# A recurrence and a highway layer on one core: two zero matmuls fewer, late outputs in other buffers, a new order of work

## The chip, the cores and the metric

The kernel runs on one core of a Trainium2 chip. The metric is device time in microseconds, the median of several executions. A core has five engines with a queue of instructions each: TensorE (PE, matmuls and transposes; PEld are its weight loads), VectorE (DVE), ScalarE (ACT), GpSimd (POOL) and SyncE (SP), which here only issues transfers. Each queue runs in its own order, and engines wait for one another by semaphores. Matrix results land in PSUM, everything else lies in SBUF.

## The reference, cut to what matters

Two steps on 4 sequences of 6336 tokens with 256 channels, in float32:

```python
sig = 1 / (1 + exp(-f_logit))
f = lower_bound + (1 - lower_bound) * sig
i = 1 - f
h = 0                                     # per sequence and channel
for t in range(S):
    h = f[:, t] * h + i[:, t] * x[:, t]   # a recurrence along the tokens
    y[:, t] = h
y = y.reshape(B * S, D)
H = maximum(y @ w_h, 0)
T = 1 / (1 + exp(-(y @ w_t + b_t)))
out = T * H + (1 - T) * y
```

Logits and x are read and the output is written once, about 26 MB each.

## The kernel before

**Units.** The 25344 tokens are cut into 28 units in the order of the tokens: units 0 and 1 of 256 tokens, 2 of 512, then 23 of 1024 (3 to 25), 26 of 512 and 27 of 256. A unit is worked in two halves of 128 channels, with channels on the partitions and tokens along the free dimension, so that the recurrence is one scan instruction per half. At a sequence's start inside a unit the scan is cut in two.

**Steps of a unit**, each a function named do_ and a letter:

- `l` and `x` load the logits and x (SP queue, 1 MB each for a full unit); six buffers each.
- `u` (ACT) takes the sigmoid of the negated logits. `b0` to `b3` (POOL, or DVE where the token has a `v`) multiply u and x, two blocks of 128 tokens at a time.
- `i` (PE) transposes u, `f` (ACT, or DVE with `v`) makes the decay from it out of PSUM. `p` (PE) transposes b.
- `s` (DVE) is the scan: it reads f and p's PSUM bank, and the last column of the scan before.
- `z` and `g` (PE) are the two matrix products. `t` (ACT) is the sigmoid of z; `d` (DVE) takes the maximum of g and the scaled y. In the kernel's algebra the weights are scaled and w_h has the identity taken off, so that the output is y scaled by `diag` plus d times t.
- `E` (POOL, pieces of 512 columns) and `e` (DVE, the rest) multiply d and t. A unit's last number says how many columns go to POOL; of a full unit's 2048 the rest goes to DVE. A POOL product is made to wait for the DVE product ahead of it, since the two share a port.
- `o` (PE) transposes back and adds, four blocks of 128 tokens at a time; `c` (ACT, or DVE with `v`) copies it to SBUF, into one of four `o` buffers of 512 KB; `w` (SP) stores it.

At the start, `pc` and `cc` turn the parameters, `wh` and `wt` load the weights, into the first `o` buffer, `WS` or `WSv` takes the identity off w_h (POOL or DVE), `WHa` and `WTa` scale the weights on ACT, `dga` makes `diag`.

**PSUM.** Two single banks (a0, a1) serve `i` and `p`; three pairs of banks (b0 to b2) serve `z`, `g`, `o`. The number behind a token's colon is its buffer. A step that takes a buffer waits for the last reader of what was in it.

**Order.** Nothing is scheduled at build time: the list `order`, a string of some 870 tokens, is read from left to right, and each token puts its instructions at the end of its engine's queue, in program order. A token `k*16` puts 16 matmuls on zeros, whose result nobody reads, into PE's queue; `p3.1*2` puts two of them ahead of that step. Eight more stand at the very start (line 178), behind a memset. The list and the units' shares come from a planner outside the kernel, so the text of the list is the whole of the schedule.

The lines of the steps: loads 281, u 293, b 301, i 307, f 316 (DVE) and 318 (ACT), p 327, scan 344, z and g 356 with 141 for the matmuls that keep their weights, t 369, d 373, e and E 378, o 397 and 398, c 405 (DVE) and 407 (ACT), w 412.

Of the kernel before, what the change touches and what calls it, by code (L numbers as in the profile page):

```python
# [77 lines left out]
g1.1:1 f4.1:4 z2.0:0 s3.0 d1.1 E2.1:1 u5:0 E1.0:2 x6:0 p4.1:0 o0.0:2 t2.0 c0.0:1 i5.0:1 z3.0:0 f5.0:1 l7:1 b5.1:2 w0.0
g3.1:1 o1.0:2 b5.0 t3.0:0 l8:2 b5.3 p4.0:1 b5.2 c1.0:2 u6:1 s4.1:0 i5.1:0 E2.0 d3.1:3 z3.1:2 b6.2:0 b6.0 f5.1:0 t3.1
s4.0 g3.0:1 d3.0 p5.1:1 i6.0:0 f6.0:3 z4.0:0 b6.1 w1.0 o2.0:2 p5.0:0 s5.1:1 i6.1:1 t4.0:1 c2.0:3 b6.3 g4.1:0 u7:2 x7:1  # L80
s5.0 z4.1:1 d4.1:0 E3.0:0 f6.1:4 l9:3 e3 g5.0:2 E3.1 d5.0:1 w2.0 g4.0:0 p6.1:1 i7.0:0 t4.1 b7.1:1 b7.0 b7.2 d4.0
z5.1:2 u8:0 E4.2:2 o3.0:1 s6.1:2 l10:4 f7.0:2 c3.0:0 p6.0:0 o3.1:0 b7.3 s6.0 z5.0:1 x8:2 t5.1:2 e4 E4.1 c3.1:1 u9:1
g5.1:2 i7.1:0 x9:3 E4.0 z6.0:0 w3.0 d5.1 p7.0:1 o4.1:2 t5.0 E5.1:1 b8.2:2 f7.1v:0 o4.0:1 p7.1:0 t6.0:0 b8.1 b8.0
c4.1:2 s7.0:3 c4.0:3 g6.0:2 z6.1:1 u10:2 g6.1:0 t6.1 b8.3 i9.0:1 s7.1 d6.0:2 i8.0:0 g7.0:1 d6.1 f9.0:1 i8.1:1 z7.1:2
z7.0:0 f8.0:4 E5.0 b9.2:0 w3.1 i10.1:0 x10:4 f8.1:3 d7.0:3 e5 e6:0 p8.0:1 o5.0:1 w4.0 t7.1:1 b9.1 b9.0 o6.1:2 f10.1:2
b9.3 p8.1:0 w4.1 t7.0 c6.1:0 s8.0:0 g7.1:0 c5.0:1 i10.0:1 l11:5 E7.0:2 E6.0 b10.1:1 o5.1:2 f10.0:0 i9.1:1 c5.1:3 s8.1
p9.0:0 z8.0:1 x11:5 b10.0 f9.1:4 b10.3 d7.1 u11:0 b10.2 s9.0:1 z8.1:2 p9.1:1 s9.1 o6.0:0 t8.0:2 l12:0 t8.1 g8.1:1
g9.0:2 w6.1 u12:1 c6.0v:2 E7.1 i11.1:1 z9.0:0 d9.0:0 i12.0:0 w5.0 f11.1:3 t9.0:0 p10.0:1 z9.1:2 g9.1:0 f12.0:1 E7.2
b11.0:2 d8.1:1 t9.1 w5.1 E7.3 i11.0:0 b11.3 o7.1:1 s10.0:2 f11.0:4 d9.1 l13:1 b11.1 p10.1:1 i12.1:0 s10.1 c7.1:0
g8.0:2 o7.0:1 b11.2 p11.0:1 u13:2 x12:0 d8.0 E9.0:1 l15:2 f12.1:0 b12.1:0 z10.0:0 s11.0:3 c7.0:1 t10.0:1 g10.1:2  # L90
g10.0:1 w6.0 z10.1:0 E9.1 x13:1 w7.1 d10.0:2 i13.0:1 E9.3 u15:0 p11.1:0 E9.2 t10.1 b12.0 l14:3 b12.3 d10.1 b12.2
b13.2:1 w7.0 x15:2 f13.0:2 s11.1 o9.0:1 e8:0 o9.1:2 i13.1:1 c9.0:3 p12.0:0 x14:3 e10:2 l17:4 b13.1 c9.1:2 f13.1:4
z11.0:1 o8.0:2 o8.1:0 p12.1:1 u14:1 c8.0:0 w9.1 z11.1:2 c8.1:1 s12.0:1 b13.0 b13.3 i14.0:0 s12.1 g11.0:0 i15.1:1
b15.1:2 t11.0:0 b15.0 f14.0:3 w9.0 b14.2:0 p13.0:0 z12.1:1 d11.0:3 t11.1 s13.0:0 f15.1:1 g11.1:2 d11.1 i15.0:1 g12.0:0
t12.1:2 b14.0 f15.0:0 l16:5 w8.0 p13.1:0 z12.0:2 w8.1 u17:2 t12.0 b14.1 o10.1:1 E11.1:1 E11.0 b14.3 x16:4 i14.1:1
E11.2 d12.0:0 s13.1 g12.1:0 g13.0:2 c10.1:2 E12.0:0 f14.1:2 o10.0:1 E11.3 p14.0:0 d12.1 b15.3 b15.2 g13.1:0 u16:1
l18:0 i16.1:1 c10.0:3 d13.0:1 o11.0:2 E12.2 w10.1 s14.0:2 z13.0:1 f16.1:4 b16.0:1 c11.0:0 w10.0 p14.1:0 d13.1 t13.0:1
i16.0:1 z13.1:2 x17:5 E13.0:2 f16.0:3 s14.1 o11.1:0 e12 p15.1:1 b16.2 t13.1 i17.1:0 b16.3 c11.1:1 E12.1 z14.0:1 b16.1
g14.0:2 w11.0 E13.1 f17.1:2 z14.1:0 s15.1:3 l19:1 E13.2 t14.0:0 p15.0:0 w11.1 d14.0:2 g14.1:1 t14.1 i17.0:1 s15.0
u18:0 x18:0 f17.0:1 o12.1:2 c12.1:2 E13.3 o12.0:0 E14.1:1 p16.0:0 p16.1:1 d14.1 o13.0:1 s16.0:1 g15.1:2 s16.1 b17.2:0  # L100
c12.0:3 c13.0:0 u19:1 g15.0:0 l20:2 i18.0:0 b17.1 d15.1:3 b17.3 e14 b17.0 f18.0:0 z15.0:1 i19.0:1 t15.0:2 i19.1:0
b18.0:2 E14.0 x20:1 g16.1:2 d15.0 f19.1:3 d16.1:0 o13.1:1 w12.1 p17.0:0 w13.0 f19.0:4 z16.1:0 g16.0:2 p17.1:1 c13.1:1
b18.1 t16.1:1 b18.3 b18.2 x19:3 s17.0:0 z15.1:1 i18.1:0 o14.1:0 u20:2 b20.2:1 d16.0 f18.1:1 t15.1 o14.0:2 p18.1:0
s17.1 z17.1:1 c14.0:2 i20.0:1 z16.0:2 l21:3 c14.1:0 t17.1:0 w13.1 e15:0 f20.0:2 g17.1:0 b20.1 z17.0:1 s18.1:2 t16.0
w12.0 p18.0:1 b20.3 t17.0 w14.0 u21:0 i20.1:0 d17.1:1 s18.0 b19.2:0 w14.1 b19.1 g17.0:2 o15.0:1 g18.0:0 d17.0 f20.1:1
b20.0 l22:4 x21:2 i21.1:1 d18.0:2 l23:5 c15.0:1 b19.0 b19.3 o15.1:2 p19.0:0 f21.1:0 e16:2 z18.0:0 E17.1:1 w15.0
p19.1:1 c15.1:3 o16.1:1 s19.0:3 z18.1:2 i21.0:0 s19.1 w15.1 E17.3 t18.0:2 c16.1:2 E17.2 g18.1:0 g19.0:1 E16.0 t18.1
o16.0:2 d18.1 p20.1:1 f21.0:4 E17.0 E18.0:0 d19.0:3 u22:2 c16.0:0 z19.0:0 p20.0:0 z19.1:1 x22:4 o17.0:2 b21.1:2
s20.1:1 b21.3 t19.0:1 b21.0 w16.1 l24:0 b21.2 o17.1:0 i22.0:1 t19.1 s20.0 e18 E19.0:2 E19.1 b22.0:0 p21.0:0 b22.3
u23:1 g19.1:1 c17.0:1 s21.0:0 b22.1 z20.0:2 c17.1:3 z20.1:0 d19.1 f22.0:3 i23.1:0 t20.0:0 x23:5 p21.1:1 g20.0:2  # L110
o18.0:1 w17.0 f23.1:1 b22.2 t20.1 c18.0:2 i22.1:0 g20.1:0 f22.1:2 w17.1 o18.1:1 s21.1 l25:1 d20.0:0 p22.0:1 d20.1
i23.0:0 w18.0 g21.1:2 E19.3 s22.0:2 x24:0 u24:0 E19.2 f23.0:4 o19.1:0 i24.1:1 b23.3:1 b23.1 c19.1:1 d21.1:1 p22.1:0
z21.0:2 g21.0:0 w19.1 e20:1 f24.1:0 s22.1 c18.1:3 w16.0 b23.0 b23.2 t21.0:2 o19.0:1 E20.2 p23.0:1 w18.1 E20.0 d21.0
g22.0:2 E20.1 z21.1:0 s23.0:3 b24.1:2 u25:2 c19.0:2 b24.3 x25:1 l27:2 i25.1:0 z22.0:1 f25.1:3 d22.0:2 t22.0:1 w19.0
x26:3 p23.1:1 i24.0:0 z22.1:2 g22.1:1 t21.1 t22.1 s23.1 b24.0 o20.0:0 d22.1 l26:3 b24.2 f24.0:2 o20.1:2 c20.1:1 e21:0
E21.0 p24.1:0 c20.0:0 E22.2:2 b25.2:0 z23.1:1 b25.0 w20.1 g23.1:2 p24.0:1 z23.0:0 s24.1:1 d23.1:3 t23.1:0 t23.0 b25.3
o21.1:1 g23.0:2 i25.0:0 s24.0 b25.1 o21.0:0 u27:1 E22.0 w20.0 d23.0 c21.1:3 g24.1:1 i27.0:1 f25.0:4 w21.1 c21.0:2
# [335 lines left out]
```

## Time and profile before

| what | value |
|---|---|
| median of 3 executions | 210.8 us (210.74 to 211.06) |
| the profiled execution | 211.13 us |
| its span (first to last instruction) | 209.3 us |
| busy: PE, DVE, ACT, POOL | 192.9, 193.1, 194.9, 174.8 us |
| moved by DMA | 78.69 MB, 376 GB/s over the span |
| granted TensorE clock | 0.994 |

A line of a timeline gives the start in us, the duration, the engine, the source line, the operation with output and inputs, their shapes and how many instructions were merged; in square brackets stands how long the engine was idle before it and what ended that. Tile names are those of the program without buffer numbers, so which unit a line belongs to follows from the list's order. A line of a stretch gives its limits, its length, the busy us of PE, PEld, DVE, ACT and POOL with their number of instructions, the granted clock, the busy share of the 16 transfer engines and their rate. The slices on the page are 40 equal parts of the span, 5.23 us each, in tenths of busy time.

### The profile page before, as it was taken

The page shows a single profiled execution, that of the slowest core. Times are in us where ns is not written, and L with a number is a line of the kernel's source. Part 1 is how long each engine was busy: PE and PEld are TensorE (multiplying, and loading weights), DVE is VectorE, ACT ScalarE, POOL GpSimd, SP SyncE. Part 2 cuts the span into 40 slices and gives each one's busy share as a digit, 9 for nine tenths or more (in the row PEclk, how much of TensorE's full clock was granted, in tenths as well). Part 3 has the DMA queues.
Part 4 walks back from the last instruction along what each step waited for, and adds up shares of the span by engine and source line. Part 5 has one row for each costly group of instructions (what it writes and reads, how often), then busy time and mean ns, then how long its engine had stood idle before and what let it go on. Part 6 is the DMA issues. An engine that isn't in the chain of part 4 may idle for free.

```text
span 209.3 us, 4671 instructions
## 1 busy us (share of the span) xinstructions
PE 192.9 (92%) x1827; PEld 132.6 (63%) x1827; DVE 193.1 (92%) x149; ACT 194.9 (93%) x194; POOL 174.8 (84%) x168
## 2 busy tenths in 40 slices
PE   7978799999998999889999999999989899999981
...
DVE  0489999999999999999999999999999999999842
ACT  4889899999999999999999999999999999997871
...
DMA  6999999999999999999999999999999999756585
GB/s 238 387 421 421 418 417 420 417 423 418 409 427 402 399 386 418 430 408 423 428 357 377 426 411 425 411 403 399 419 421 344 332 368 345 293 205 232 193 340 223
DMA packets 15982, 78.69 MB, mean 376 GB/s; under 512 B 1748, under 2 KB 2264, under 8 KB 10072
## 3 DMA queue, kind: packets, MB, share of 16 engines
...
q8 instruction: 14, 0.23, 0.5%
q14 instruction: 8, 0.07, 0.1%
...
## 4 chain that ended last, share of the span: by engine, by line
PE 32%; DVE 24%; issue 4%; ACT 3%; DMA 3%; DVEq 0%; ACTq 0%
DVE y L344 14%; DVE d L373 8%; PE g L356 5%; PE bT L327 4%; PE op L398 4%; PE g L141 4%; PE op L397 4%; PE z L356 4%; PE z L141 4%; PE uT L307 3%; DMA out_dram<-o 3%; DVE e L378 2%; ACT o L407 1%; ACT u L293 1%; ACT f L318 0%
## 5 line engine op out<-in xcount | busy, mean ns | idle before, releaser
L301 POOL TENSOR_TENSOR bv<-u,x 128x512 bf16<-128x512 f16 x95 | 108.6, 1173 | 13.9 <-DVE e L378 7.6
L344 DVE TENSOR_TENSOR_SCAN y<-f,y,bT 128x1024 bf16<-128x1024 f16 (+5 forms) x54 | 106.7, 1991 | 1.4 <-PE bT L327 1.0
L378 POOL TENSOR_TENSOR e<-d,t 128x512 bf16<-128x512 bf16 (+1 forms) x60 | 65.9, 1118 | 9.8 <-DVE e L378 7.3
L373 DVE SCALAR_TENSOR_TENSOR d<-y,ncc,g 128x1024 bf16<-128x1024 bf16 (+2 forms) x56 | 62.8, 1142 | 3.8 <-PE g L356 3.4
L369 ACT ACTIVATE t<-z,bt 128x1024 bf16<-128x1024 f32 (+2 forms) x56 | 57.2, 1043 | 1.7 <-PE z L141 0.9
L318 ACT ACTIVATE f<-uT,ncc 128x1024 f16<-128x1024 f16 (+2 forms) x53 | 55.5, 1060 | 2.1 <-PE uT L307 1.9
L293 ACT ACTIVATE u<-l 128x2048 f16<-128x2048 f32 (+2 forms) x28 | 48.5, 1732 | 3.3 <-DMA l<-in_f_logit_dram 3.3
L407 ACT COPY o<-op 128x1024 f32<-128x1024 f32 (+1 forms) x49 | 48.5, 1019 | 1.8 <-DMA out_dram<-o 0.6
L398 PE MATMUL op<-ident_b,e 128*128 128x128 bf16 x396 | 48.7, 219 | 0.8 <-DVE e L378 0.8
L397 PE MATMUL op<-diag,y 128*128 128x128 f16 x396 | 48.7, 219 | 0.4 <-ACT o L407 0.4
L398 PEld LDWEIGHTS <-e 128*128 128x128 bf16 x396 | 44.1, 113 | 4.1 <-issue 1.1
L397 PEld LDWEIGHTS <-y 128*128 128x128 bf16 x396 | 44.2, 113 | 2.4
L356 PE MATMUL z<-y,w_sb 128*128 128x512 bf16 (+1 forms) x112 | 39.2, 367 | 1.5 <-ACT o L407 0.6
L356 PE MATMUL g<-y,w_sb 128*128 128x512 bf16 (+1 forms) x112 | 39.4, 368 | 1.0 <-ACT t L369 0.6
L327 PE MATMUL bT<-ident_f,bv 128*128 128x128 f32 x198 | 32.1, 278 | 4.4 <-DVE y L344 2.3
L141 PE MATMUL g<-y,w_sb 128*128 128x512 bf16 x92 | 34.8, 379 | 0.0
L141 PE MATMUL z<-y,w_sb 128*128 128x512 bf16 x92 | 34.8, 379 | 0.0
L307 PEld LDWEIGHTS <-u 128*128 128x128 f16 x396 | 26.1, 98 | 13.2 <-issue 5.6
L307 PE MATMUL uT<-ident_h,u 128*128 128x128 f16 x396 | 30.9, 220 | 3.1 <-ACT f L318 1.3
L356 PEld LDWEIGHTS <-w_sb 128*128 128x128 f16 x224 | 21.7, 98 | 17.4 <-issue 1.2
L141 PEld LDWEIGHTS <-w_sb 128*128 128x128 f16 x184 | 17.9, 97 | 18.6 <-issue 4.1
L327 PEld LDWEIGHTS bT<-ident_f,bv 128*128 128x128 f32 x198 | 22.0, 141 | 11.2 <-POOL bv L301 3.4
...
## 6 DMA issues: line engine op xcount, KB each, us to landing
...
l<-in_f_logit_dram SPq DMA_DIRECT2D x23, 1024.0 KB, 10.2
...
```

What stands on the lines that cost most here:

```text
L141: return pe.add_instruction(mybir.InstMatmult(name=nc.get_next_instruction_name(), start_tensor_calc=start, stop_tensor_calc=stop, tile_si ...
L301: shared(pin(e.tensor_mul(st[n]["bv"][:, k].rearrange("p d j -> p j d"), st[n]["u"][:, q:q + 2], st[n]["x"][:, q:q + 2])), not eng)
L307: pin(nc.tensor.transpose(uT[:, j * P:(j + 1) * P], st[n]["u"][:, j, h * P:(h + 1) * P], ident_h))
L318: pin(nc.scalar.activation(to, of, AF.Identity, scale=ncc[:, h:h + 1], bias=1.0))
L327: pin(nc.tensor.transpose(words[:, k:k + g * (P - 1) + 1:g], pair, ident_f))
L344: pin(nc.vector.tensor_tensor_scan(y[:, c:e], st[n]["f", h][:, c:e], st[n]["bT", h][:, c:e], 0.0 if fresh else carry[h], op0=ALU.mult, op1 ...
L356: pin(nc.tensor.matmul(p[:, a:e], w, half(n, "y", ki)[:, a:e], start=ki == 0, stop=ki == NH - 1))
L369: pin(nc.scalar.activation(half(n, "t", m), st[n]["z", m][:, :tokens(n)], AF.Sigmoid, bias=bt[:, m:m + 1]))
L373: pin(nc.vector.scalar_tensor_tensor(half(n, "d", m), half(n, "y", m), ncc[:, m:m + 1], st[n]["g", m][:, :tokens(n)], op0=ALU.mult, op1=AL ...
L378: shared(pin(eng.tensor_mul(st[n]["e"][:, a:e], st[n]["d"][:, a:e], st[n]["t"][:, a:e])), eng is nc.gpsimd)
L397: pin(nc.tensor.matmul(o, half(n, "y", h)[:, cols], diag[:, h], start=True, stop=False))
L398: pin(nc.tensor.matmul(o, half(n, "e", h)[:, cols], ident_b, start=False, stop=True))
```

## The change

Three things change.

1. At line 178 six matmuls on zeros stand where eight stood.
2. A buffer number in the list may now be a name. `c23.1:x3` puts its output into buffer 3 of x's six. The copies of units 23 to 27 do so: c23.1 to x3, c23.0 to x5, c24.0 to x0, c24.1 to x1, c25.0 to x4, c25.1 to x2, c26.0 to x5, c27.0 to x3. Such an output tile has x's full size, of which the copy and the store use the first half at most. Earlier units keep the four `o` buffers.
3. The list is another one, and so are the columns that POOL takes of each unit's product: 27392 in all instead of 29440. The units and their sizes stay. Of the steps that may run on two engines: `WSv` becomes `WS` (DVE to POOL); b1.0 and b3.0 go from DVE to POOL; f0.1 goes from DVE to ACT, f1.0 and f2.0 from ACT to DVE; on DVE stand the copies c1.0 and c25.0 where c6.0 and c27.0 stood. The loads' order at the start goes from l0 l3 wh x0 l1 l2 x1 wt x2 x3 l4 x4 l5 to l0 l3 x0 l1 wh l2 x1 x2 x3 wt l4 x4 l5. The matmuls on zeros in the list are 26 instead of 24.

The diff, with the list cut to its start and end:

```diff
     units = [
         (0, 128, 2, 0, 'y', 4, 512),
-        (0, 128, 2, 256, 'y', 4, 512),
+        (0, 128, 2, 256, 'y', 4, 0),
         (0, 128, 4, 512, 'y', 4, 1024),
...
-        (0, 128, 8, 21504, 'y', 4, 1280),
-        (0, 128, 8, 22528, 'y', 4, 256),
-        (0, 128, 8, 23552, 'y', 4, 1536),
+        (0, 128, 8, 21504, 'y', 4, 2048),
+        (0, 128, 8, 22528, 'y', 4, 1280),
+        (0, 128, 8, 23552, 'y', 4, 0),
         (0, 128, 4, 24576, 'y', 4, 512),
         (0, 128, 2, 25088, 'y', 4, 256),
     ]
     order = """
-l0:0 pc:0 l3:1 wh:0 cc u0:0 u3:1 i0.1:0 i0.0:1 k*16 x0:0 l1:2 f0.1v:0 f0.0:1 l2:3 WSv b0.0v:0 u1:2 p0.0:1 x1:1 p0.1:0
-k*3 s0.1:0 WHa s0.0 i1.1:0 k*3 u2:0 wt f1.1v:2 i1.0:0 x2:2 i2.1:1 f1.0:3 b1.0v:1 f2.1:4 g0.1:1 x3:3 b2.1:2 p1.0:0 b2.0
-i3.1:1 l4:4 WTa s1.0:1 p1.1:0 s1.1 g0.0:2 d0.0:0 d0.1 z0.1:0 f3.1:0 i3.0:0 i2.0:1 z1.1:2 t0.1:0 b3.2v:0 f2.0:1 z0.0:0
-p2.1:1 b3.0v f3.0:3 z1.0:1 p2.0:0 t0.0 b3.1 x4:4 s2.1:2 g1.0:0 b3.3 t1.1:1 s2.0 p3.1*2:1 u4:2 dga l5:5 E0.0:0 x5:5
+l0:0 pc:0 l3:1 u0:0 i0.0:0 x0:0 i0.1:1 k*12 cc f0.1:0 l1:2 wh:0 f0.0:1 l2:3 x1:1 x2:2 b0.0v:0 WS p0.1:0 u3:1 u1:2
+p0.0:1 k*2 s0.0:0 i3.1:1 s0.1 i1.0:0 k*2 f1.0v:2 x3:3 i1.1:0 k*3 WHa f3.1:3 f1.1v:4 b1.0:1 u2:0 p1.0:1 g0.0:1 s1.0:1
+p1.1:0 k*2 i3.0:1 g0.1:0 s1.1 wt i2.0:0 g1.0:2 f3.0:1 i2.1:1 b2.0:2 WTa f2.1:0 b2.1 d0.0:0 f2.0v:2 p2.0:0 z1.1*2:1
+d0.1 b3.0:0 b3.1 g1.1:0 p2.1:1 t1.1:0 l4:4 x4:4 d1.0:1 s2.0:2 z1.0:2 d1.1 b3.2v dga z0.1:1 t1.0 u4:2 z0.0:0 t0.1:1
+s2.1 b3.3 p3.1*3:0 l5:5 t0.0 i4.0:1 f4.0:4 e1:0 b4.0:1 b4.3 g2.1:2 g2.0:1 z2.1:0 i4.1:1 t2.1:2 b4.1 s3.1:3 x5:5 p3.0:0
...
-t25.0:1 i26.0:1 z25.1:1 i27.1:0 E23.1 d25.1:1 E23.2 d25.0 w22.1 f26.0:2 e24 p26.0:1 t25.1 o23.1:2 o23.0:0 f27.1:4
-x27:2 p26.1:0 o24.0:1 c23.1:3 o24.1:2 E25.0:2 b27.0:2 s26.0:2 c23.0:2 p27.0:1 s26.1 g26.1:0 c24.0:1 c24.1:0 g26.0:1
-e25 p27.1:0 z26.0:2 w23.1 t26.0:0 E25.2 E25.1 d26.1:2 d26.0 z26.1:0 o25.0:1 w23.0 t26.1 c25.0:3 s27.1:3 o25.1:2 s27.0
-g27.0:0 z27.1:1 E26.0:1 w24.0 d27.0:3 e26 z27.0:0 c25.1:2 t27.0:2 o26.0:2 t27.1 g27.1:1 d27.1 E27.0:0 w24.1 w25.0 e27
-w25.1 c26.0:1 w26.0 o27.0:0 c27.0v:0 w27.0
+c22.0:2 s25.0 E23.1 o22.1:1 g24.1:2 i26.1:1 f26.0:1 p26.0:0 c22.1:3 d24.0:0 f26.1:0 g25.0:1 d24.1 b27.0:0 E23.2
+p26.1:1 w21.1 w21.0 z25.1:0 z25.0:2 t25.1:1 d25.0:1 o23.1:1 s26.0:2 t25.0 o23.0:0 g25.1:2 w22.0 E24.0:1 s26.1 c23.1:x3
+p27.0:1 c23.0:x5 e24 g26.0:1 E24.2 w22.1 i27.1:0 d25.1 o24.0:0 d26.0:2 f27.1:4 z26.0:2 c24.0:x0 E24.1 p27.1:0 t26.0:0
+o24.1:1 e25:0 z26.1:0 w23.0 w23.1 w24.0 E26.0:2 s27.0:3 c24.1:x1 o25.0:2 o25.1:1 t26.1 s27.1 w24.1 g26.1:0 c25.0v:x4
+w25.0 c25.1:x2 d26.1 z27.0:2 z27.1:1 g27.0:0 t27.0:2 w25.1 e26 o26.0:2 d27.0:3 t27.1 c26.0:x5 g27.1:1 d27.1 E27.0:1
+e27 w26.0 o27.0:0 c27.0:x3 w27.0
 """
...
-        return pool.tile(shape, dtype, tag=f"{name}{slot}", name=name)
+        return pool.tile(shape, dtype, tag=slot if str(slot)[:1].isalpha() else f"{name}{slot}", name=name)
...
-    for _ in range(8):
+    for _ in range(6):
         nc.tensor.matmul(once["idle"][:, :512], zeros[:, :P], zeros, start=True, stop=True)
...
-        o = sb([P, 4, D], FP32, "o", slot)
+        o = sb([P, NB if slot[:1] == "x" else 4, D], FP32, "o", slot)
```

More of the change, by code (lines that the diff above doesn't have):

```diff
@@ L78 @@
[L78 to L117, printed above, removed]
@@ new lines @@
+E3.2 z4.1:1 b6.2 f7.0:1 u8:0 d4.1:1 w1.0 s5.0 l10:4 o2.0:0 b6.0 c2.0:3 i6.1:1 f6.1:2 i7.1:0 x10:3 x9:4 g5.1:0 w2.0
+i6.0:1 d4.0 t4.1 f6.0:4 z5.0:1 f7.1v:0 b7.2:1 d5.1:0 e4:1 p6.0:0 e3 l11:5 i8.1:1 u9:1 o3.0:0 l12:0 b7.0 b7.1 b7.3
+o3.1:2 s6.0:2 E4.0 f8.1:3 b8.1:2 t5.0:2 c3.0:0 p6.1:1 g5.0:1 i9.0:0 c3.1:2 s6.1 z6.1:0 p7.1:1 d5.0 w3.1 o4.0:2 f9.0:4
+p7.0:0 u10:2 c4.0:1 w4.0 b8.0 t6.1:0 g6.0:1 s7.1:3 i8.0:1 z5.1:2 d6.0:2 f8.0:2 E4.1 z6.0:0 i10.1:1 b8.2 g6.1:1 t5.1
+s7.0 b8.3 o4.1:2 t6.0 E5.0:2 E5.1 e5 p8.1:0 f10.1:0 c4.1:3 i9.1:1 d6.1 w3.0 b9.2:0 z7.1:0 g7.0:1 s8.1:1 d7.0:3 f9.1:1
@@ new lines @@
+g12.0:2 E12.2:0 o10.0:1 c10.1:2 f15.0:1 g13.0:0 b16.2:1 d12.0 i16.1:1 w8.0 w8.1 p14.0:0 c10.0:3 x17:5 z13.0:1 E12.1
+E12.0 o11.1:2 f16.1:3 d13.0:1 b16.3 p14.1:1 s14.0:2 l18:0 u17:1 z13.1:0 t13.0:1 i17.1:0 E12.3 w10.1 b16.1 b16.0
+c11.1:0 t13.1 g13.1:1 s14.1 f17.1:2 d13.1 o11.0:2 w10.0 l20:1 p15.0:1 g14.1:0 i16.0:0 s15.0:3 b17.0:2 c11.0:1 z14.1:1
+z14.0:2 p15.1:1 f16.0:4 p16.0:0 E13.1:1 b17.1 d14.1:2 o12.0:0 t14.1:0 b17.2 s15.1 w11.1 E13.0 g14.0:1 b17.3 t14.0
+o12.1:2 u18:0 d14.0 i17.0:1 c12.0:2 E13.2 f17.0:1 l19:2 w11.0 s16.0:0 E14.2:2 x18:0 w12.0 c12.1:3 g15.0:1 g15.1:0
```

58 lines of the change are left out of this document (43 added, 15 removed).

## The prediction

> **What bounds the kernel now.** I read the page first, then the stretches of the span, then the timeline of each engine at the two ends, and last the groups by form, which give the durations. On the page, the slices say that four engines and the transfers are full at once, and that only the ends are not.
>
> ```profile
> PE   7978799999998999889999999999989899999981
> DVE  0489999999999999999999999999999999999842
> ACT  4889899999999999999999999999999999997871
> DMA  6999999999999999999999999999999999756585
> ```
>
> The stretches (busy us of PE, PEld, DVE, ACT, POOL, then clock, transfer share, GB/s) make it sharper: in the body VectorE and ScalarE do not miss a tenth of a microsecond, and in the last ten VectorE falls to 2.09 of 5 while the transfers are busy again.
>
> ```profile
> 120.00:130.00 10.00, 9.65 (x105) 7.04 (x103) 10.00 (x8) 10.00 (x10) 9.18 (x9) 1.00 1.02 419
> ...
> 195.00:200.00 5.00, 4.93 (x58) 3.67 (x57) 4.42 (x7) 4.20 (x6) 4.60 (x5) 1.00 0.69 266
> 200.00:205.00 5.00, 3.65 (x50) 2.90 (x47) 2.09 (x5) 3.92 (x6) 1.48 (x2) 1.00 0.91 362
> ```
>
> So the time is: start of the unbroken VectorE work, plus that work, plus its holes in the tail, plus the last store. The head on the timeline (start, duration, engine, line):
>
> ```profile
> 7.69 0.78 DVE L301 TENSOR_TENSOR bv<-u,x 128x512 bf16<-128x512 f16 x1 [1.86 <-DMA x<-in_x_dram]
> ...
> 10.75 0.73 DVE L301 TENSOR_TENSOR bv<-u,x 128x512 bf16<-128x512 f16 x1
> ...
> 12.09 0.75 DVE L344 TENSOR_TENSOR_SCAN y<-f,y,bT 128x256 bf16<-128x256 f16 x1 [0.61 <-PE bT L327]
> 12.43 2.29 POOL L301 TENSOR_TENSOR bv<-u,x 128x512 bf16<-128x512 f16 x2 [4.55 <-DMA x<-in_x_dram]
> ...
> 19.00 2.34 DVE L344 TENSOR_TENSOR_SCAN y<-f,y,bT 128x1024 bf16<-128x1024 f16 x1
> ```
>
> From 12.09 (s1.0) inputs no longer hold VectorE; 19.00 is s3.1, the first full-size scan. The tail, VectorE first, then ScalarE:
>
> ```profile
> 197.84 1.41 DVE L373 SCALAR_TENSOR_TENSOR d<-y,ncc,g 128x512 bf16<-128x512 bf16 x2 [0.58 <-PE g L356]
> ...
> 201.55 0.48 DVE L373 SCALAR_TENSOR_TENSOR d<-y,ncc,g 128x256 bf16<-128x256 bf16 x1 [1.02 <-PE g L356]
> ...
> 204.15 0.48 DVE L373 SCALAR_TENSOR_TENSOR d<-y,ncc,g 128x256 bf16<-128x256 bf16 x1 [1.79 <-PE g L356]
> ...
> 205.58 0.69 DVE L405 COPY o<-op 128x512 f32<-128x512 f32 x1 [0.55 <-PE op L398]
> ```
>
> ```profile
> 200.55 1.02 ACT L407 COPY o<-op 128x1024 f32<-128x1024 f32 x1 [0.41 <-DMA out_dram<-o]
> 201.78 1.01 ACT L407 COPY o<-op 128x1024 f32<-128x1024 f32 x1 [0.21 <-DMA out_dram<-o]
> ```
>
> VectorE's holes there are 0.58 + 1.02 + 1.79 + 0.55 and 0.1 between d27.1 and e27, 4.05 in all; two of ScalarE's are output copies waiting for an output buffer still being stored.
>
> **Account of the profiled execution.** Span 209.3: s3.1 at 19.0; VectorE work and its 0.15 of small holes; the 4.05; 3.03 from the end of the last copy (206.27) to the end. Work is thus 209.3 - 19.0 - 0.15 - 4.05 - 3.03 = 183.07. This execution took 211.13, so 1.83 lies around the span, and it is 0.33 above the median 210.8; I carry the difference over to 210.8.
>
> **Part 1, amounts.** Counting the list's tokens by form with the means of the groups by form, VectorE goes from 202.46 to 202.78 us (two bv of 0.74 go to GpSimd, one f of 512 comes from ScalarE at about 0.76, the e shares grow by 1.04), ScalarE from 213.04 to 212.35, GpSimd from 178.5 to 176.4. (These exceed the busy time because neighbours overlap by 0.07 to 0.1.) Zero matmuls: 8 + 24 become 6 + 26, no change in number. The transfers and their 78.4 MB stay.
>
> **Part 2, head.** Landings follow bytes queued ahead: with the page's 238, 387 and 421 GB/s per slice of 5.23 us, the queue has moved 1.24, 3.27 and 5.47 MB at 5.2, 10.5 and 15.7 us, and x0 (1.83 MB through it) landed 0.94 later than that, x2 (3.67 MB) 1.0 later. In the new issue order x0 has 1.57 MB: 7.0 instead of 7.69. wh moves from 7.01 to 8.4, wt, now behind x2 and x3, from 11.1 to 14.9, x2 from 12.43 to 11.75, x3 to 14.2; x1 keeps 2.88 MB and lands at 10.4 in both. So the first scans start 0.7 earlier, and that gain dies at s1.0: its b1.0 is moved to GpSimd (1.17 instead of 0.73), behind WS there, 10.4 to 11.6, and with the 0.6 that before took from bv to scan, s1.0 starts at 12.05 against 12.09. VectorE idles about 1.7 before it. From there to s3.1: s1.0, s1.1, d0.0, f2.0v, d0.1, d1.0, s2.0, d1.1, b3.2v, s2.1, e1 = 1.35 + 0.4 + 0.69 + 0.8 + 1.2 + 0.4 + 0.68 + 1.2 + 0.36 = 7.1, and 0.15 for d1.1: PE stands at z1.1 until ScalarE's WTa, waiting for wt, ends at 15.8, and g1.1 comes after. s3.1 at 19.3: **+0.3**. Ends: -0.3 (x1's landing is the estimate that carries it) and +0.8 (d1.1 and s2.1 each late by PE's queue behind z1.1, where p2.1 also stands). VectorE work behind s3.1 is 0.16 more (192.02 against 191.86): **+0.16**. ScalarE reaches u4 at 17.8 instead of 17.26, but u5 must wait for l5, at 23.49 in both; its work left is then the same (179.9 after u5), so its lateness is covered by that landing.
>
> Six zero matmuls instead of eight let prmT go 0.85 earlier (0.43 each in the row 1.19 to 4.78); f0.1 and f0.0 then fit in ScalarE's 2.25 wait for l3. If that cover fails, it costs ScalarE 0.3 ahead of l5, still hidden. What eight may have bought is the clock: the zero matmuls ran 0.43 apart, those from 5.31 on 0.23 apart. The Trainium skill (TensorE: Matmul & The Clock Gate, Part 1) says that the clock opens only after a busy window of about 3.4 us, which runs freely, so a thinner start may open it a window later. The sum by that page would have k*12 take 12 x 0.43 = 5.2 instead of 2.7 us, ending near 9.7. By rows of this case alone: even at 0.43 apart to the end of k*12, p0 would slip by under 2 us, s0 by as much, and 1.7 of it falls in the hole before s1.0. I take 0, with 0.3 as the other end.
>
> **Part 3, tail.** From s25.1 VectorE has 18.55 us to e27 in the new list (c25.0v, 1.13, and all of e25, 1.15, among it). I walk the queues with 0.87 for a full z, g or o, 0.45 for those of 512, 1.06 for t, 0.95 for c. If ScalarE begins u26 together with s25.1: c22.1 ends at 6.5 and frees the bank of g25.0, d25.0 starts 0.45 late; t25.0 ends at 10.65, o23.0 and g25.1 follow to 12.0, d25.1 waits 0.55; d26.1 0.1; d27.0 0.05; d27.1 waits 0.8, since o26.0 stands ahead of g27.1 on PE and needs e26. Sum 2.0. With ScalarE 1 us ahead: 1.15. The places of both engines in their sums put it between; I take 1.5. Nothing waits for a store now: c23.1 to c25.1 use x3, x5, x0, x1, x4, x2, whose readers ended long before, and c26.0 reuses x5 7 us after w23.0 was issued, against 5.5 for the store that the chain shows and 6.9 median. Then o27 0.55 and its copy, now on ScalarE, 0.60 instead of VectorE's 0.69 (which was in the work). So 4.05 becomes 1.5 + 1.15: **-1.4**. Ends: -1.85 (idle 1.15, e25 hiding more) and +0.1 (idle 3.0, near the present 3.5 before o27: only the place of the last copy changed).
>
> **Part 4, body.** The list between is new. A VectorE that has 0.15 of holes in 185 us can lose nothing more than that, so the bounds are -0.1 and +2.0, the latter what ScalarE has as holes between 20 and 180 in the same trace. Summed work shows where: a scan's lead over its f is, where thinnest, -3.2 (s18.1) and -3.7 (s25.0) before, and -3.5 (s18.1), -3.7 (s21.0), -4.1 (s23.0) after, in one scale in which ScalarE runs 4.6 to 6 us ahead. Some 1 to 2 us stay. Nearest to VectorE's own row, I take **+0.4**.
>
> Sum: 0.3 + 0.16 - 1.4 + 0.4 = -0.54. 210.8 - 0.5 = 210.3.
>
> **Rivals.**
> (a) ScalarE falls behind and VectorE stalls (slower). Place: u7 and u8, which come 5 and 4 us of ScalarE work earlier. l7 has 11.0 MB through the queue against l5's 7.9: 23.5 + 3.1 / 0.418 = 31.0, its turn 31.4; l8 36.0 against 36.4. Margins of 0.4 where u7 had 2 and u8 2.7. ScalarE has no idle to recover, so its lag meets the leads of about 1 at s18.1, s21.0, s23.0. It decides from about 1 us of lag; at 2 to 2.5 VectorE loses 1.5 instead of 0.4: 211.4. For: transfers at 1.0 until 180 us. Against: l6 had the same margin and ScalarE showed no wait.
> (b) The tail gains little, for PE is 4.93 of 5 busy there: idle 2.5 gives -0.4, the sum +0.46, and with a clean body 0: 210.8 to 211.2. For: three of the four holes are put down to PE's g. Against: those g wait in turn for copies that waited for stores.
> (c) All ends well: s3.1 0.3 early, body clean, tail -1.85: -2.0, 208.8.
> (d) The change in buffers does nothing, the direct wait being only 0.62: in (b).
>
> **Chances.** By 0.2%, 0.42 us, a measurement here can hardly tell a change. Forecast 0.40 (209.5 to 210.4), (c) 0.08, (b) 0.25, of which 0.18 lie within 0.42 and 0.07 above, (a) with worse heads, 0.27. Faster 0.48, same 0.18, slower 0.34. The range leaves out the far half of (c) and the upper part of (a), whose bound of 2.0 for the body with a head of +0.8 and no tail gain would reach 213: 209.0 to 212.2. The forecast's own range is 209.5 to 210.4.
>
> **What would show it.** s1.0 at about 12.05 with a hole ahead of it; s3.1 at 19.0 to 19.8; WTa waiting for wt; no ScalarE copy waiting for a store after 190; VectorE holes after s25.1 of 1 to 2 us, the greatest before d27.1; under 0.5 us of holes between. Wrong if ScalarE waits for l at u7 to u10, or scans wait for bT by an f; or if holes before d remain 3 us.

## The result

| | median | executions |
|---|---|---|
| before | 211.00 us (210.68 to 211.27) | 22 |
| after | 211.38 us (211.11 to 212.93) | 22 |

The ratio is 1.0027, with an interval of 1.0017 to 1.0038. By the medians the change costs 0.38 us, where 0.5 us less was forecast. The sign was wrong, the time is inside the range given.

The profiled execution of after took 212.73 us (span 210.9). In it TensorE's clock falls to half for 3.4 us near 26 us. By their times and mean clocks (0.99) three of the 22 executions have that fall (212.57, 212.73, 212.93); the other 19 lie between 211.11 and 211.82, with a median of 211.36. So this trace shows two things, of which only one is in the median, and I use the first experiment (a_keep below, which prevents that fall and changes nothing else) as the undisturbed after.

### The profile page after: what moved, and what is told of

The parts are those of the page before. It is cut to its first block, busy times and chain, and to the rows that moved or that the text cites. A ratio compares the mean times of both kernels' runs of the same rounds, so it can differ in the third digit from the quotient of the medians.

```text
span 210.9 us, 4661 instructions
## 1 busy us (share of the span) xinstructions
PE 194.0 (92%) x1827; PEld 133.5 (63%) x1827; DVE 193.7 (92%) x148; ACT 194.9 (92%) x193; POOL 172.8 (82%) x167
## 2 busy tenths in 40 slices
DMA packets 15982, 78.69 MB, mean 373 GB/s; under 512 B 1748, under 2 KB 2264, under 8 KB 10072
## 4 chain that ended last, share of the span: by engine, by line
PE 49%; DVE 14%; ACT 12%; DMA 10%; POOL 6%; issue 5%; SPq 1%; DVEq 0%; ACTq 0%
DVE y L344 10%; DMA l<-in_f_logit_dram 7%; PE op L398 7%; PE op L397 7%; PE z L356 6%; PE g L356 6%; PE uT L307 6%; PE bT L327 6%; PE g L141 6%; PE z L141 5%; ACT t L369 4%; ACT u L293 4%; POOL bv L301 3%; ACT o L407 3%; DVE d L373 3%
## 5 line engine op out<-in xcount | busy, mean ns | idle before, releaser
L301 POOL TENSOR_TENSOR bv<-u,x 128x512 bf16<-128x512 f16 x97 | 111.2, 1174 | 18.1 <-DVE e L378 10.6
L378 POOL TENSOR_TENSOR e<-d,t 128x512 bf16<-128x512 bf16 (+1 forms) x57 | 61.8, 1101 | 7.7 <-DVE d L373 5.1
L407 ACT COPY o<-op 128x1024 f32<-128x1024 f32 (+1 forms) x49 | 49.6, 1039 | 3.1 <-PE op L398 2.6
L398 PE MATMUL op<-ident_b,e 128*128 128x128 bf16 x396 | 49.3, 220 | 1.6 <-POOL e L378 0.8
L397 PE MATMUL op<-diag,y 128*128 128x128 f16 x396 | 49.2, 219 | 0.1
L356 PE MATMUL z<-y,w_sb 128*128 128x512 bf16 (+1 forms) x112 | 40.3, 376 | 1.7 <-ACT o L407 0.5
L141 PE MATMUL z<-y,w_sb 128*128 128x512 bf16 x92 | 35.6, 387 | 0.0
L307 PE MATMUL uT<-ident_h,u 128*128 128x128 f16 x396 | 31.6, 221 | 3.8 <-DVE y L344 2.4
L327 PE MATMUL bT<-ident_f,bv 128*128 128x128 f32 x198 | 31.4, 278 | 2.7 <-POOL bv L301 1.3
```

The source lines that it names most:

```text
L141: return pe.add_instruction(mybir.InstMatmult(name=nc.get_next_instruction_name(), start_tensor_calc=start, stop_tensor_calc=stop, tile_si ...
L301: shared(pin(e.tensor_mul(st[n]["bv"][:, k].rearrange("p d j -> p j d"), st[n]["u"][:, q:q + 2], st[n]["x"][:, q:q + 2])), not eng)
L307: pin(nc.tensor.transpose(uT[:, j * P:(j + 1) * P], st[n]["u"][:, j, h * P:(h + 1) * P], ident_h))
L327: pin(nc.tensor.transpose(words[:, k:k + g * (P - 1) + 1:g], pair, ident_f))
L356: pin(nc.tensor.matmul(p[:, a:e], w, half(n, "y", ki)[:, a:e], start=ki == 0, stop=ki == NH - 1))
L378: shared(pin(eng.tensor_mul(st[n]["e"][:, a:e], st[n]["d"][:, a:e], st[n]["t"][:, a:e])), eng is nc.gpsimd)
```

## The profile after

The slices of after, to be read against those of before: the body is as full as it was, PEclk has a 7 in the sixth slice, and the transfers are thin at the end (8 6 5 5 4 9 5).

```profile
PE   6888798889998899999999989999999999999990
DVE  1489969999999999999999999999999999999970
ACT  4969789999999999999999999999999999996872
...
PEclk9999979999999999999999999999999999999999
DMA  6999999999999999999999999999999998655495
```

Stretches of after (limits, length, busy us of PE, PEld, DVE, ACT, POOL, clock, transfer share, GB/s). From 25 to 30 us the mean clock is 0.66 and VectorE works 3.19 of 5 us. From 200 to 205, where before had 2.09 of 5 for VectorE, after has 4.17.

```profile
25.00:30.00 5.00, 4.73 (x29) 2.60 (x27) 3.19 (x3) 3.69 (x5) 4.31 (x5) 0.66 1.01 419
120.00:130.00 10.00, 9.01 (x95) 6.65 (x94) 10.00 (x7) 10.00 (x10) 10.00 (x10) 1.00 1.01 417
...
195.00:200.00 5.00, 5.00 (x64) 4.04 (x63) 4.90 (x7) 4.25 (x6) 2.71 (x3) 1.00 0.35 137
200.00:205.00 5.00, 4.71 (x61) 3.73 (x59) 4.17 (x7) 3.71 (x6) 1.50 (x2) 1.00 0.94 369
```

VectorE's timeline of after at the head (start, duration, engine, line, operation): b0.0 earlier by 0.85, a hole ahead of s1.0 at 11.85, s3.1 at 19.16.

```profile
6.84 0.74 DVE L301 TENSOR_TENSOR bv<-u,x 128x512 bf16<-128x512 f16 x1 [1.93 <-DMA x<-in_x_dram]
...
11.85 1.39 DVE L344 TENSOR_TENSOR_SCAN y<-f,y,bT 128x256 bf16<-128x256 f16 x2 [0.64 <-PE bT L327]
...
19.16 2.35 DVE L344 TENSOR_TENSOR_SCAN y<-f,y,bT 128x1024 bf16<-128x1024 f16 x1
```

A little later in the same timeline stands the stall that the clock makes: s4.0 waits 1.78 us for its transposed input.

```profile
25.91 2.34 DVE L344 TENSOR_TENSOR_SCAN y<-f,y,bT 128x1024 bf16<-128x1024 f16 x1
30.03 2.35 DVE L344 TENSOR_TENSOR_SCAN y<-f,y,bT 128x1024 bf16<-128x1024 f16 x1 [1.78 <-PE bT L327]
```

The tail of after, VectorE and then ScalarE. The 4.05 us of holes are down to about 1.4, the greatest ahead of d27.1, and no copy waits for a store. The last copy, now on ScalarE, ends at 206.77 + 0.58 = 207.35, and the span ends 3.59 us later. In before the same distance was 3.08. (The page rounds spans to a tenth, which is why the prediction has 3.03. These distances, here and below, go by the trace's own times.)

```profile
205.32 0.48 DVE L373 SCALAR_TENSOR_TENSOR d<-y,ncc,g 128x256 bf16<-128x256 bf16 x1 [0.80 <-PE g L356]
205.93 0.29 DVE L378 TENSOR_TENSOR e<-d,t 128x256 bf16<-128x256 bf16 x1
```

```profile
205.14 1.01 ACT L407 COPY o<-op 128x1024 f32<-128x1024 f32 x1 [0.84 <-PE op L398]
206.77 0.58 ACT L407 COPY o<-op 128x512 f32<-128x512 f32 x1 [0.62 <-PE op L398]
```

Two theories of the loss come from this. One needs a word first: the instructions of an engine are themselves brought in by transfers, and the page lists 14 such packets of 16 KB beside the data (`q8 instruction: 14, 0.23, 0.5%` in before). **Late engine:** an instruction block fetched in the tail by one of the 16 transfer engines puts that engine behind, and the last store waits for it. **Stores too close:** the last two stores follow one another more closely than before, and the last one is slow for that. For the fall of the clock the theory is a window in which TensorE had too little to do.

## The experiments

### TensorE's clock near 26 us: a_keep and a_eight

a_keep puts five zero matmuls ahead of p4.1, at 23.1 us, where TensorE waits anyway. a_eight puts the two zero matmuls at the head back.

```diff
-... t2.0 p4.1:1 b5.2:2 ...
+... t2.0 p4.1*5:1 b5.2:2 ...
```

```diff
-    for _ in range(6):
+    for _ in range(8):
```

> The changed kernel with five matmuls on zeros put ahead of p4.1, in a stretch (22 to 25 us) where TensorE is half idle; nothing else moves. Theory (the TensorE clock falls to half at about 25.7 us in some executions because the stretch before it is too idle, and such an execution loses 1.3 us): the executions of 212.5 to 212.9, 3 of 22 for the changed kernel, are gone, all lie within 211.0 to 211.8, the granted clock is 1.00 from 25 to 30 us, and scan s4.0 waits under 0.5 us where it waited 1.78. The median falls by less than 0.1, since most executions do not have the drop. Rival (the hole comes from the list, the clock only goes with it): s4.0 still waits over 1 us and the median stays at 211.4. Rival 2 (the drop costs every execution something): the median falls by 0.3 or more, to 211.0.

> The changed kernel with eight matmuls on zeros at the start, as before. Theory (the two matmuls are hidden: the first scans wait for x1 anyway): within 0.2 of the changed kernel, 211.2 to 211.6, with prmT about 0.4 later and s1.0 at the same 11.85. Rival (six were too few for the clock at the start): faster by over 0.2 us, and TensorE's matmuls before 8 us run closer together.

a_keep: 211.32 us (211.12 to 211.99, 12 executions; one lies above the 211.8 expected), 1.0013 [1.0002, 1.0025] of before, clock whole. a_eight: 211.31 us (211.15 to 213.25), 1.0026 [1.0007, 1.0045]; two of its 12 executions have the fall, the profiled one among them. The stretches that decide are the 3.41 us ahead of 25.8 us, counted in steps of 3.413 us from the moment at which the clock opened (5.22 in after, 5.31 in before, 5.34 in a_keep, 5.41 in a_eight). After, with the window that follows; then a_eight, before and a_keep:

```profile
22.32:25.73 3.41, 1.91 (x18) 1.18 (x17) 3.35 (x3) 2.80 (x3) 3.12 (x3) 0.99 1.02 423
25.73:29.11 3.38, 3.38 (x15) 1.58 (x13) 2.52 (x2) 2.35 (x3) 2.98 (x3) 0.50 1.01 419
```

```profile
22.48:25.89 3.41, 1.88 (x18) 1.17 (x17) 3.35 (x3) 2.78 (x3) 3.10 (x3) 1.00 1.02 423
```

```profile
22.38:25.79 3.41, 2.17 (x21) 1.39 (x20) 3.37 (x4) 2.85 (x3) 3.41 (x4) 1.00 1.00 416
```

```profile
22.41:25.82 3.41, 2.82 (x23) 1.66 (x22) 3.36 (x3) 2.84 (x3) 3.12 (x3) 1.00 1.02 423
```

TensorE busy for 1.91 and 1.88 us of such a window: the next one runs at half clock. Busy for 2.17 or 2.82: it does not. In a_keep s4.0 waits 0.19 us instead of 1.78:

```profile
28.53 2.35 DVE L344 TENSOR_TENSOR_SCAN y<-f,y,bT 128x1024 bf16<-128x1024 f16 x1 [0.19 <-PE bT L327]
```

Since after falls in only 3 of 22 executions, and a_keep's median is after's (211.32 against 211.36 for the undisturbed 19), the fall is not what makes the change slower. Nor are the two zero matmuls.

### The part on buffers alone: a_obuf and b_xbuf

a_obuf is after with its eight last copies in o buffers; b_xbuf is before, with its own list, and x's buffers for those copies.

```diff
 after -> a_obuf
-c23.1:x3 c23.0:x5 c24.0:x0 c24.1:x1 c25.0v:x4 c25.1:x2 c26.0:x5 c27.0:x3
+c23.1:0  c23.0:1  c24.0:2  c24.1:3  c25.0v:0  c25.1:1  c26.0:2  c27.0:3
 before -> b_xbuf
-c23.1:3  c23.0:2  c24.0:1  c24.1:0  c25.0:3  c25.1:2  c26.0:1  c27.0v:0
+c23.1:x4 c23.0:x5 c24.0:x0 c24.1:x1 c25.0:x3 c25.1:x2 c26.0:x4 c27.0v:x5
```

> The changed list, with the outputs of the last five units back in the four o buffers, taken in turn. Theory (the change of buffers takes a true wait away, but the wait was short): ScalarE's or VectorE's copies at the tail wait for stores again, 0.3 to 1.5 us in all, and the time is 0.2 to 1.0 above the changed kernel, 211.6 to 212.4. Rival (the buffers do nothing): within 0.2 of the changed kernel, 211.2 to 211.6. Rival 2 (x's buffers are themselves what hurts): faster than the changed kernel by over 0.2.

> The list of before, with only the change of buffers: the eight output copies of units 23 to 27 in x4, x5, x0, x1, x3, x2, x4, x5. Theory (the two waits for stores, 0.41 and 0.21 us, stand on the path to the end): 0.3 to 0.8 faster than before, and the holes of VectorE in the tail fall from 4.05 by as much. Rival (other waits take their place, as TensorE is 4.93 of 5 busy there): within 0.2 of before. In neither is it slower.

a_obuf: 212.87 us (212.42 to 213.79, 6 executions), 1.0093 [1.0071, 1.0114], above the 211.6 to 212.4 expected. By their mean clocks (0.983 to 0.988) three of its six executions have the fall; the median of the other three is 212.64. b_xbuf: 210.94 us (210.70 to 211.39), 0.9998 [0.9988, 1.0007]. VectorE in the tail of a_obuf, one copy:

```profile
201.90 1.22 DVE L405 COPY o<-op 128x1024 f32<-128x1024 f32 x1 [2.05 <-PE op L398]
```

and in that of b_xbuf, in which no copy waits for a store any more:

```profile
198.22 1.41 DVE L373 SCALAR_TENSOR_TENSOR d<-y,ncc,g 128x512 bf16<-128x512 bf16 x2 [0.58 <-PE g L356]
...
201.94 0.48 DVE L373 SCALAR_TENSOR_TENSOR d<-y,ncc,g 128x256 bf16<-128x256 bf16 x1 [1.01 <-PE g L356]
...
204.19 0.48 DVE L373 SCALAR_TENSOR_TENSOR d<-y,ncc,g 128x256 bf16<-128x256 bf16 x1 [1.44 <-PE g L356]
```

The copy of a_obuf waits 2.05 us; the row names TensorE, whose last op for it was done at 201.1, so the last part of the wait is the store in that buffer. With before's list the buffers win nothing: the 1.44 in front of the last d, where before has 1.79, stands in the profiles of b_six and b_split5 as well, which keep the o buffers, and the rest stays. Compared without the fall of the clock (212.64 against 211.36), the buffers are worth 1.3 us to the new list, which was laid out for them, and nothing measurable to the old one.

### From the last copy to the end: a_no26 and a_split2

a_no26 is a_keep without the store of unit 26. a_split2 is a_keep (with its five zero matmuls ahead of p4.1) with every zero matmul of the list cut into two of 256 columns: 31 instruction pairs (weight load and matmul) more.

```diff
 a_keep -> a_no26
-e27 w26.0 o27.0:0 c27.0:x3 w27.0
+e27 o27.0:0 c27.0:x3 w27.0
```

```diff
 a_keep -> a_split2
-        for k in range(extra[0]):
+        for k in range(2 * extra[0]):
+            a, e = k % 2 * 256, min(k % 2 * 256 + 256, 512)
...
-                pin(again(t[:, :512], zeros[:, :P], zeros, True, True))
+                pin(again(t[:, a:e], zeros[:, :P], zeros[:, a:e], True, True))
```

> a_keep without the store w26.0: the 512 rows of unit 26 are not written. Theory (one engine behind by its instruction block): the queue is empty for over 1 us before the last store, the engine has caught up, and the last store ends 3.0 us after the last copy: time about 210.7. If the late engine is late by the last store's own shape or place, 3.6 and 211.3.

> The kernel after with four zero matmuls more ahead of p4.1 (as in a_keep) and each zero matmul of the list cut into two of 256 columns: 31 instructions more on TensorE, in the same time. Theory (instruction block): TensorE's last 16 KB of instructions are fetched by one transfer engine, in a_keep at 198.4 us, while the store queue is full; that engine stays about 0.6 us behind through the last stores and ends the span late. 31 matmuls more bring the fetch to about 196.3 us, where the transfers are less full, so the engine catches up: from the end of the last copy to the end of the span 3.0 us instead of 3.6, time 0.5 to 0.6 below a_keep's 211.32, that is 210.7 to 210.8. Rival (the last two stores themselves are slow, since they follow one another closer than in before): 3.6 as in a_keep, time 211.3.

a_no26: 210.64 us (210.53 to 211.45, 12 executions), 0.9990 [0.9981, 0.9998]; last copy to end 2.97. a_split2: 211.53 us (211.42 to 212.04, 5 executions), 1.0036 [1.0023, 1.0049]; last copy (206.04 + 0.58) to the end of the span 3.01. Both gave the 3.0 of the late engine, not the 3.6 of the stores; the time of a_split2 is a miss all the same (210.7 to 210.8 was expected). In a_split2 w26 and w27 follow one another as in a_keep, so closeness is out. The last copy of a_keep, from which its 3.60 counts, and the transfers at the end, in stretches of 0.5 us:

```profile
205.22 0.58 ACT L407 COPY o<-op 128x512 f32<-128x512 f32 x1 [0.62 <-PE op L398]
...
207.00:207.50 0.50, 0.00 (x0) 0.00 (x0) 0.00 (x0) 0.00 (x0) 0.00 (x0) 0.50 0.90 340
207.50:208.00 0.50, 0.00 (x0) 0.00 (x0) 0.00 (x0) 0.00 (x0) 0.00 (x0) 0.50 0.08 29
208.00:208.50 0.50, 0.00 (x0) 0.00 (x0) 0.00 (x0) 0.00 (x0) 0.00 (x0) 0.50 0.01 4
```

The end of a_split2:

```profile
208.00:208.50 0.50, 0.00 (x0) 0.00 (x0) 0.00 (x0) 0.00 (x0) 0.00 (x0) 1.00 0.57 209
```

A share of 0.08 is little more than one engine of 16: in a_keep one works on alone, while the store, and with it the span, waits. What was moved is the last fetch of 16 KB of TensorE's instructions, which the trace lists as packets of their own: one engine spends 0.96 us on it at 198.4 in a_keep, and 0.95 us at 195.8 in a_split2, before the stores fill the queue.

The traces hold more direct evidence. Each load and each store reports sixteen arrivals, and the trace keeps the time of each one. In a_keep the sixteenth arrival of a transfer is at most 0.1 us behind the fifteenth until the first block is fetched, at 20.6. From the next load on it is 1.3 us behind, and it stays so for seven transfers. After the block at 198.4 it is 1.97 us behind, and of the last store fifteen arrivals are in by 207.93, the sixteenth at 208.51. In a_split2 all sixteen arrive within 0.2 us (208.58 to 208.74). So it is one engine, it is late from the block on, and it makes up the 0.6 us.

The Trainium skill (DMA: Bandwidth & Descriptors, Queues, rings and completion order) says that a transfer is split over up to 16 engines, and that each engine takes turns, packet by packet, between the queues that have work for it. The same page (Why a DMA increments its semaphore by 16 and not by 1) says that the transfer is complete only when each engine has posted; the trace agrees, with 0.58 us between the last arrival and the other fifteen in a_keep.

The time of a_split2 still went up, since it has the last copy 0.8 us later. In its profile the clock opened at 8.63 instead of 5.34, and the head's zero matmuls, at half speed until then, ended at 9.57, near the 9.7 that the prediction worked out for a late opening; how much of the 0.8 this makes wasn't separated from the finer matmuls.

### The other direction: a_split4 and b_split5

The same cut into four pieces in a_keep (93 pairs more), and into five in before (96 more), to call for one more block of instructions late.

> As a_split2, but each zero matmul of the list cut into four of 128 columns: 93 instructions more. Theory: counting 129 matmuls between fetches, the last fetch of a_keep moves to about 190 us, where it is made good, but one more block may be needed, at about 201.5 us; if it is fetched, one engine ends late by 0.6 us or more (3.6 to 4.0 from last copy to end, time 211.3 or above); if it isn't, 3.0 and 210.8. Rival (stores too close): 3.6 and 211.3 in either case.

> The kernel before with each of the 24 zero matmuls of its list cut into five of about 103 columns: 96 instructions more. Theory: an additional block of TensorE's instructions is then fetched at about 200.3 us, in the full stores, and the kernel before gets the late engine that it did not have: from the end of the last copy to the end 3.5 instead of 3.03, time up by about 0.5 to 211.5 (a small change at the head may come on top). If the block is not behind it: 3.03 and 211.0.

a_split4: 212.45 us (212.32 to 212.77, 5 executions), 1.0076 [1.0064, 1.0088]. The block came at 202.3, and from the last copy (207.06) to the end it took 3.82, inside the 3.6 to 4.0 expected of the late engine; the sixteenth arrival of the last store is 0.81 late. b_split5: 212.16 us (211.62 to 212.18, 5 executions), 1.0051 [1.0039, 1.0063], but from the last copy to the end 2.96, where 3.5 was expected. The block came at 203.0, not at 200.3, in a stretch in which the transfers nearly stood still (from 202.8 to 203.8). The arrivals show one engine 0.5 to 0.6 us late in the three stores that follow, and level again in the last two: the lag was made good before the end. What the run lost, it lost before the tail: s25.1 at 186.27 instead of 184.78. Its clock fell, too, from 18.97 to 22.39, behind a window with TensorE busy for 1.79. By their mean clocks (0.990 to 0.991) three of its five executions have that fall; the other two took 211.62 and 211.84.

```profile
15.56:18.97 3.41, 1.79 (x17) 1.11 (x16) 2.85 (x4) 2.51 (x5) 1.37 (x2) 1.00 1.01 420
18.97:22.39 3.42, 3.42 (x24) 2.34 (x22) 3.13 (x3) 2.73 (x5) 3.17 (x4) 0.50 1.02 422
```

### Moving the block elsewhere: a_pad and b_six

a_pad is a_keep with 30 small zero matmuls in the body; b_six is before with six zero matmuls at the head.

```diff
 a_keep -> a_pad, in do_p
         words = bT.bitcast(FP32)
+        for _ in range(1 if 8 <= n <= 22 else 0):
+            pin(nc.tensor.matmul(words[:, :64], zeros[:, :P], zeros[:, :64], start=True, stop=True))
```

> a_keep with one matmul on zeros of 64 columns ahead of each step p of the units 8 to 22: 30 matmuls more on TensorE, none of them at the head. Theory (late engine): the last 16 KB of instructions are fetched at about 196 us, before the stores of the tail fill the queue, as in a_split2, and the head is that of a_keep, as it was not in a_split2. From the last copy to the end 2.95 to 3.05 us, time 0.5 to 0.7 below a_keep's 211.3: 210.7 to 210.8, 0.1% under the kernel before. Rival: the matmuls themselves delay the body, which has TensorE busy 9.65 of 10 us: s25.1 later than 184.4 by up to 1 us and no gain.

> The kernel before with six zero matmuls at the head instead of eight: part 1 of the change alone. Theory: no change, 210.9 to 211.0, since a_eight, which undoes it in the kernel after, gave 211.31 against 211.38. Rival (the two matmuls hold the clock's busy window open): TensorE's clock opens 3.4 us later, as in the profile of a_split2, and the time rises by 0.5 to 0.8.

a_pad: 210.97 us (210.89 to 211.90, 12 executions), 1.0004 [0.9995, 1.0012]: 0.35 under a_keep, and level with before, not 0.1% under it. Its last fetch is at 194.9, and its last copy (206.21) stands 3.03 from the end; in the stretch 207.50 to 208.00, where a_keep shows 0.08, most engines still work side by side, and the sixteen arrivals of the last store lie within 0.2 us:

```profile
207.50:208.00 0.50, 0.00 (x0) 0.00 (x0) 0.00 (x0) 0.00 (x0) 0.00 (x0) 1.00 0.78 287
```

Of the 0.6 won, 0.4 is paid back by s25.1, which starts at 184.79 (a_keep 184.36); 0.1 of that is the head's. So the theory held for the end. The rival's later s25.1 came about too, but whether the added matmuls or the moved blocks cost the other 0.3 was not separated. b_six: 210.89 us (210.69 to 211.41, 11 executions), 1.0001 [0.9993, 1.0010]: part 1 alone is worth nothing.

### The matmuls at the head instead: a_head and c_head

The 32 pairs are put where TensorE has nothing else to do, once in a_keep, once in after.

```diff
 a_keep -> a_head, after -> c_head, in busy
+            elif k >= 8:
+                for a in range(0, 512, 57):
+                    e = min(a + 57, 512)
+                    pin(again(t[:, a:e], zeros[:, :P], zeros[:, a:e], True, True))
```

> a_keep with the last four of the twelve zero matmuls of k*12 cut into nine pieces each of 57 columns or fewer: 32 matmuls more, all of them at the head, where TensorE has nothing else to do, in the same 2.7 us. Theory (late engine, and the 0.4 us that a_pad lost by s25.1 due to its matmuls in the body): the last 16 KB of instructions come at about 196 us, from the last copy to the end 3.0 us, s25.1 at 184.4 as in a_keep, time 210.7 (0.6 under a_keep, 0.1% under the kernel before). If a_pad's lost 0.4 us is due to the moved instruction blocks themselves and not to its matmuls, s25.1 comes at 184.8 and the time is 211.0.

> The kernel after with the same cut of four of its zero matmuls and nothing else (p4.1 without zero matmuls ahead). Theory: as a_head where TensorE's clock holds, 210.7 to 210.8, and 1.3 to 1.6 us more in the executions in which the clock falls for 3.4 us at about 25.7 us; of 12 executions one to three of that kind.

Both were slower: a_head 211.98 us (211.46 to 213.90, 12 executions), 1.0054 [1.0032, 1.0076], c_head 212.79 us (211.75 to 213.21, 7 executions; an eighth, of 392.65, is unexplained and left out), 1.0074 [1.0051, 1.0097]. The end came out as expected: 3.02 and 3.01 from the last copy. The loss is at the head, and ScalarE's timeline shows it, in a_keep and then in a_head:

```profile
17.45 1.91 ACT L293 ACTIVATE u<-l 128x2048 f16<-128x2048 f32 x1
```

```profile
18.80 1.91 ACT L297 ACTIVATE u<-l 128x2048 f16<-128x2048 f32 x1 [1.20 <-DMA l<-in_f_logit_dram]
```

The first of TensorE's blocks is fetched at 16.6 instead of 20.6 us. Of l4, for which u4 waits, all sixteen arrivals are in at 17.25 in a_keep; in a_head fifteen are in at 17.24 and the sixteenth at 18.71. It is the late engine again, now in front of a load. TensorE then waits 1.50 us for u4, is busy for 1.40 us of the window from 18.42 to 21.83, and the clock falls for the next window, which the five matmuls of p4.1 come too late to prevent:

```profile
18.42:21.83 3.41, 1.40 (x12) 0.89 (x13) 3.09 (x3) 3.03 (x4) 1.09 (x2) 1.00 1.01 418
21.83:25.25 3.42, 3.42 (x17) 2.25 (x16) 0.88 (x2) 2.37 (x3) 3.42 (x4) 0.50 1.00 417
```

By their mean clocks (0.987 to 0.989), 4 of 12 executions of a_head and 4 of 7 of c_head have such a fall; for c_head one to three of 12 were expected. Without them the medians are 211.81 and 211.80, still 0.45 over the undisturbed after (211.36). No version here beats both kernels.

## Why the prediction was wrong

Its steps against the undisturbed after (a_keep: 211.18 us profiled, span 209.4):

| | before | forecast | measured |
|---|---|---|---|
| s1.0 starts | 12.09 | 12.05 | 11.96 |
| s3.1 starts | 19.00 | 19.3 | 19.27 |
| wait ahead of d27.1 | 1.79 | 0.8 | 0.79 |
| e27 ends | 205.03 | | 204.67 |
| last copy ends | 206.27 | 205.73 | 205.80 |
| from there to the end | 3.08 (3.03 in the prediction) | 3.03 | 3.60 |
| sixteenth arrival of the last store | 208.45 | | 208.51 |
| the other fifteen | 208.33 | | 207.93 |

The 205.73 is the forecast's span, 209.3 - 0.54, less 3.03.

**The step that failed** is the last one, "3.03 from the end of the last copy (206.27) to the end", which the account of before put in and no part of the change touched. It measured 3.60. The last copy does end 0.47 us earlier than before's, near the 0.54 forecast, but the end of the span stays where it was (209.40 against 209.35). I had costed the last store by its size and its place in the queue, and not asked which other packets the 16 engines carry. The end is the later of two things: the last copy plus about 3.0 us, and the work of the one engine that fetched the last block of TensorE's instructions.

That engine was late in before as well: its block comes at 196.6, and its arrival is 2.56 us behind the other fifteen in the store that lands next. From there to the end it lands one store of 512 KB every 1.2 us, in both kernels, while the others pause for the copies. In before one engine works nearly alone in the first of these stretches, and all end nearly together:

```profile
205.00:205.50 0.50, 0.41 (x5) 0.28 (x5) 0.03 (x1) 0.00 (x0) 0.00 (x0) 1.00 0.07 25
...
207.50:208.00 0.50, 0.00 (x0) 0.00 (x0) 0.00 (x0) 0.00 (x0) 0.00 (x0) 0.50 0.70 262
```

The late engine ended 0.12 us after the rest in before, so the 3.03 looked like a price of the last store. The new list brings the copies earlier and leaves the late engine's end where it was. The time of the fetch alone doesn't decide: in b_xbuf the block comes at 198.2, as late as in a_keep (198.4), but its last copy is at 206.31, and the end comes 2.96 later. a_no26, a_split2, a_pad, a_head and c_head took the 0.6 away, a_split4 made it 0.8. That the late engine is the one with the instruction block is read from the times, since the trace names no engines: the sixteenth arrival falls behind just after a block is fetched.

The two waits of before's copies for stores (0.41 and 0.21), which part 3 takes away, are this engine's too: they end with sixteenth arrivals at 200.45 and 201.68, while the other fifteen were in by 197.89 and 199.18. So is the wait of a_obuf's copy (201.82 against 199.95).

The 0.92 between forecast (-0.54) and result (+0.38) is 0.52 at the end, 0.07 at the last copy, 0.27 from the two executions compared (before's profiled one lies 0.13 above its median, a_keep's 0.14 below its own), and 0.06 between the medians of after and a_keep.

**Part 2, head: right.** x0, s1.0 and s3.1 came within 0.2 us, with the hole ahead of s1.0, and WTa waited for wt (0.25 us, to 14.77). One detail was wrong without a price: VectorE has no hole at d1.1. The zero matmuls at the head were taken at 0, and a_eight and b_six show no difference. That u5 waits for l5 until 23.5 in both kernels came true (23.49 and 23.63), but not by the bytes ahead of it alone: fifteen of l5's arrivals are in by 22.2 in both, and the sixteenth, behind the first block, at 23.41 and 23.53.

**Part 3, tail: right in kind.** No copy waits for a store, the greatest hole is ahead of d27.1, and VectorE's holes sum to 1.4 us. Yet from s25.1 to the last copy a_keep takes 21.44 and before 21.49: the holes are filled by work that before had done earlier, as the forecast had it, with 0.2 more than it summed (18.55 + 1.5 + 1.15 = 21.2).

**Part 4, body: right where the clock holds.** s25.1 starts at 184.36, 0.42 ahead of before's. Between s3.1 and s25.1 VectorE has 0.93 of holes in a_keep and 0.59 in before: 0.34 more, where 0.4 was forecast. (The prediction read 0.15 for before; it passed over a hole of 0.30 at 27.65 and several under 0.1.) The rival (a), ScalarE late at u7 and u8, did not come about: neither u waits for its load. Its time, 211.4, is the one measured, for none of its reasons. Nor is it rival (b): the tail's idle time fell to 1.4 us, not to 2.5. (c) is out.

**What it did not see** is the fall of the clock near 26 us in 3 of 22 executions. The prediction weighed the Trainium skill's rule (TensorE: Matmul & The Clock Gate, Part 1) for the opening only. The page also says that the clock goes back to half after an idle window of about 3.4 us; the trace shows the same length (3.41 us), but a window in which TensorE was busy for 1.91 us.
